# Filler order and the reversed copy: Fourier products behind the products with v, rows reversed in 16 column blocks

## The chip, the cores and the metric

The kernel runs on one core of one Trainium2 chip. The metric is the device time of one execution in microseconds (us). The engines are named as in the profile: PE is TensorE (PEld its weight loads), DVE is VectorE, ACT is ScalarE, POOL is GpSimd, SP is SyncE, which issues most of the DMAs.

## The reference: what is computed

Inputs are q, k, v of shape (4 batches, 8 heads, 576, 64). Everything is float32.

```python
scores = q @ k.T / 8                    # per batch and head, 576 x 576
scores = where(scores >= max - tau, scores, -1e9)
attn = softmax(scores);  x = (attn @ v) # heads side by side: (4, 576, 512)
u = x + real(fft(fft(x, axis=1), axis=2))
un = layernorm(u)
y = u + relu(un @ w_ch1) @ w_ch2        # 512 -> 2048 -> 512
gate = sigmoid(causal_conv5(y))
out = (gate * (y @ w_val)) @ w_out
```

## The kernel before, in words

**Attention.** Two heads make a pair; 4 batches of 4 pairs are 16 pairs. A pair has nine tiles of 128 query rows, and two tiles make a round, so there are 72 rounds. In a round PE makes the scores (`s`, L573), DVE takes the row maxima (L585) and their threshold (L588), ACT the exponentials (L592), DVE the masked probabilities and their sums (`p`, L602), POOL divides them (L609), and two rounds later PE transposes them (`t`, L643), from where ACT copies them to `m` (L652). The score buffer is free again when DVE's mask has read it, so the next scores of PE wait for the mask two tiles back.

**Fillers.** All other work of PE is put between these as filler: generators stand in five queues. `q_prep` transposes keys and queries of the next pair (L258, L268, L277). `q_tail` transposes the last 64 probability columns (L623). `q_mean` is two products for the first layer norm (L1115). `q_pv` is the products with v (L318), whose result `xt` is then folded (`g_fold`, L331) and stored to DRAM as `xs`. `q_fft` is the Fourier transform of one batch as matrix products (`g_fft`, L372), in two stages: `cdh`/`sdh` products, then `csh`/`ssh` products of 290 columns. `filler` (L678) is called twice in a round with a budget of nominal nanoseconds; `fill` (L524) takes the first queue in the order `QORD` (L47, L484) whose head is ready, and stays with one generator until it yields a name or a condition. So `QORD` alone decides which of two ready fillers stands first.

**Forced fillers.** The probability rows stand in 4 buffers. Before DVE's mask of a new row block, `emit_mask` (L595) calls `force` (L557): while the tail transposes of the block four back are not issued, it runs fillers in the same order, and the mask of DVE then waits for those transposes of PE.

**Fourier rows in reverse order.** The second half of the Fourier rows mirrors the first. `reverse` (L368) copies rows in reverse order from DRAM to DRAM with one DMA of SP: 255 rows of `xs` to `xr` when a batch is folded, and 127 and then 128 rows of `ur` to `u_d` when its sums are made (`g_add`, L449). A row has 576 floats; the DMA walks column blocks outermost, rows within.

**After attention.** When the attention loop ends, a cycle (`CYCLE`, L43) mixes what is left of the fillers with the first chunk of the MLP: `h` products (L1068) of 16 blocks of weights and `c` products (L1084). The weights come as 64-bit words and are converted in steps on DVE, ACT and POOL (L96 to L106); 18 of the 32 pieces were converted during attention, stored in DRAM as `e_h`, `e_l`, and are loaded by SP (`w0h`, ..., L863) when room becomes free. The other chunks of the MLP and the gate follow.

Of the kernel before, what the change touches and what calls it, by code (L numbers as in the profile page):

```python
# [43 lines left out]
STORE = 2  # L44
SPENT = 2
EARLY = 18
QORD = (1, 0, 4, 2, 3)  # L47
SPARE = 1.5
CHUNKS = (512,384,384,512,512)
BEHIND = 1  # L50
# [84 lines left out]
def attention_fft(tc, right, ps_f, a, u_d, dram, conv_w, hooks):  # L135
    nc = tc.nc
    PE, DVE, ACT, POOL, SP = nc.tensor, nc.vector, nc.scalar, nc.gpsimd, nc.sync
    left, right1 = ExitStack(), ExitStack()
    with ExitStack() as right2, ExitStack() as right2b, ExitStack() as right3, ExitStack() as right4, ExitStack() as scores, ExitStack() as turned:
# [227 lines left out]

        def reverse(dst, src):  # L368

            SP.dma_start(out=dst.rearrange("r (o s) -> o r s", o=2), in_=src.rearrange("r (o s) -> o r s", o=2))  # L370

        def g_fft(b):  # L372
            yield lambda: b * NP + NP - 1 in folded
            xs = xs_d.pop(b)
            rev = dram.tile([DM // 2, S], F32, name=f"xr{b}")
            SP.dma_start(out=rev[0:1], in_=xs[256:257])
            reverse(rev[1:256], xs[511:256:-1])
            boh = fft_p.tile([128, 3, DM // 2], F32R, tag="boh", name="boh")
            bol = fft_p.tile([128, 3, DM // 2], F32R, tag="bol", name="bol")
# [69 lines left out]
        def g_add(b, j, x, xr, dd, sm, ny):  # L449
            up = slice(0, HALF + 1)  # L450
            dn = slice(S - 1, HALF, -1)
            md = slice(1, HALF)
            POOL.tensor_tensor(out=x[:, up], in0=x[:, up], in1=dd[:, up], op=ALU.add)
            yield
            POOL.tensor_tensor(out=x[:, dn], in0=x[:, dn], in1=sm[:, md], op=ALU.add)
            SP.dma_start(out=u_d[b][j * 128:(j + 1) * 128], in_=x)
            yield
            if j == 0:
                ACT.activation(dd[0:1], ny, AF.Copy)
                ACT.activation(sm[0:1], ny, AF.Copy)  # L460
                yield
            POOL.tensor_tensor(out=xr[:, up], in0=xr[:, up], in1=sm[:, up], op=ALU.add)
            yield
            POOL.tensor_tensor(out=xr[:, dn], in0=xr[:, dn], in1=dd[:, md], op=ALU.add)
            rev = dram.tile([128, S], F32, name=f"ur{b}_{j}")
            SP.dma_start(out=rev, in_=xr)
            if j == 0:
                SP.dma_start(out=u_d[b][256:257], in_=rev[0:1])
                reverse(u_d[b][511:384:-1], rev[1:128])
            else:  # L470
                reverse(u_d[b][384:256:-1], rev)
            added.add((b, j))
# [10 lines left out]
        q_prep, q_tail, q_pv, q_fft, q_mean = deque(), deque(), deque(), deque(), deque()  # L483
        queues = [(q_prep, q_tail, q_mean, q_pv, q_fft)[i] for i in QORD]  # L484
        hooks.update(side=side, fillers=q_mean, fill_tile=fill_tile, done=done)
# [1058 lines left out]
```

## Time and profile before

| | us |
|---|---|
| median of 3 runs | 930.17 (928.85 to 931.04) |
| the profiled execution | 930.04, its span 928.3 |
| PE busy | 878.8 (95%) |
| DVE busy | 555.0 (60%) |
| ACT busy | 452.0 (49%) |
| POOL busy | 368.4 (40%) |
| chain that ended last | PE 36%, issue 7%, POOL 3% |

A group row of the profile gives line, engine, operation, output and inputs, the number of instructions, busy time, mean time of one in ns, and the idle time just ahead of them with what ended it. Matmuls are pipelined, so a busy PE is not PE at its peak. Idle time of an engine that is not the bottleneck costs nothing. The score and v products in float32 show two matmuls in the trace for one of the program.

### The profile page before, as it was taken

To read this page: it belongs to the slowest core of one execution; us is meant where nothing else is said; L and a number is where in the kernel's file an instruction comes from. 1 tells how busy PE (TensorE), PEld (TensorE's weight loads), DVE (VectorE), ACT (ScalarE), POOL (GpSimd) and SP (SyncE) were. 2 spreads that over 40 slices of the span, in tenths; PEclk is the share of its full clock that TensorE was granted. 3 is DMA by queue.
4 is the path that set the end of the run, shared out by engine and by line. 5 is a ranking of instruction groups with operands and counts; after the bars stand their busy time and mean duration, and the time that the engine had idled before them with its cause. 6 is when DMAs were issued, how large, how long until landed. Compare 5 with 4: busy or idle time off the path is not lost. (4 is left out here: it accounts for less than half of the span.)

```text
span 928.3 us, 14888 instructions
## 1 busy us (share of the span) xinstructions
PE 878.8 (95%) x5232; PEld 697.3 (75%) x5232; DVE 555.0 (60%) x1240; ACT 452.0 (49%) x915; POOL 368.4 (40%) x451
## 2 busy tenths in 40 slices
PE   5988898999999999899998999999999999999998
PEld 3555576657655675578876999999888878898897
DVE  6888788878877866515597445444121375525750
ACT  4778786767777765625455133233123122214432
POOL 2465544675377637612554422321110201047421
PEclk9999999999999999999999999999999999999999
DMA  6775545557455731496349723211300230333111
GB/s 154 194 191 136 154 123 149 142 174 196 138 169 162 205 101 54 137 344 208 128 152 347 278 91 126 94 71 55 110 1 1 68 125 1 116 112 130 67 44 69
DMA packets 135283, 123.34 MB, mean 133 GB/s; under 512 B 87222, under 2 KB 97702, under 8 KB 135208
## 3 DMA queue, kind: packets, MB, share of 16 engines
q1 hardware_dynamic: 126760, 97.57, 34.0%
q0 software_dynamic: 6960, 24.49, 8.5%
q8 instruction: 42, 0.69, 0.3%
q10 hardware_dynamic: 1488, 0.33, 0.2%
q14 instruction: 33, 0.27, 0.1%
HBM read 89.85 MB, written 37.22 MB: 137 GB/s over the span
## 5 line engine op out<-in xcount | busy, mean ns | idle before, releaser
L1072 DVE SCALAR_TENSOR_TENSOR hl<-h,hh 128x512 fp32r<-128x512 f32 (+1 forms) x80 | 50.9, 637 | 196.5 <-ACT hh L1071 196.5
L1071 ACT ACTIVATE hh<-h 128x512 fp32r<-128x512 f32 (+1 forms) x80 | 44.3, 554 | 250.0 <-PE h L1068 249.8
L609 POOL TENSOR_SCALAR p<-p,su 128x576 f32<-128x576 f32 x144 | 110.4, 773 | 91.7 <-DVE su L699 73.3
L602 DVE SCALAR_TENSOR_TENSOR p<-s,thr,e 128x576 f32<-128x576 f32 x144 | 112.6, 815 | 40.5 <-ACT e L592 21.0
L573 PE MATMUL s<-kt,qt 64*128 64x288 f32 (+1 forms) x640 | 100.3, 444 | 25.0 <-DVE p L602 25.0
L1084 PE MATMUL c<-hl,w1h 128*128 128x512 f32 (+1 forms) x320 | 118.0, 369 | 0.6 <-DVE hl L1072 0.6
L1084 PE MATMUL c<-hh,w1h 128*128 128x512 f32 (+1 forms) x320 | 118.0, 369 | 0.0
L1084 PE MATMUL c<-hh,w1l 128*128 128x512 f32 (+1 forms) x320 | 118.0, 369 | 0.0
L592 ACT ACTIVATE e<-s,neg 128x576 f32<-128x576 f32 x144 | 99.5, 737 | 28.7 <-DVE neg L585 28.1
L585 DVE TENSOR_REDUCE neg<-s 128x1 f32<-128x576 f32 x144 | 101.3, 744 | 15.1 <-PE s L573 15.1
L573 PEld LDWEIGHTS s<-kt,qt 64*128 64x128 f32 (+1 forms) x640 | 46.0, 177 | 66.5 <-issue 24.4
L652 ACT ACTIVATE m<-t 128x512 f32<-128x512 f32 x144 | 84.7, 588 | 6.8 <-PE t L643 6.7
L1068 PE MATMUL h<-unh,w0l 128*128 128x512 f32 (+1 forms) x320 | 79.3, 369 | 4.7 <-POOL w0l L106 4.5
L318 PE MATMUL f<-m,v 128*64 128x320 f32 (+1 forms) x512 | 81.3, 419 | 1.5 <-ACT m L652 1.2
L643 PE MATMUL t<-ident,p 128*128 128x128 f32 x576 | 79.0, 281 | 2.6 <-POOL xf L348 1.9
L1068 PE MATMUL h<-unh,w0h 128*128 128x512 f32 (+1 forms) x320 | 79.3, 369 | 1.8 <-DMA w0h<-e_h 1.0
L1068 PE MATMUL h<-unl,w0h 128*128 128x512 f32 (+1 forms) x320 | 79.2, 369 | 0.0
L643 PEld LDWEIGHTS t<-ident,p 128*128 128x128 f32 x576 | 65.5, 143 | 18.1 <-issue 10.3
L1068 PEld LDWEIGHTS h<-unh,w0l 128*128 128x128 f32 x320 | 58.4, 188 | 13.7 <-POOL w0l L106 5.8
L1084 PEld LDWEIGHTS c<-hl,w1h 128*128 128x128 f32 x320 | 60.4, 189 | 8.7 <-DVE hl L1072 1.0
L1068 PEld LDWEIGHTS h<-unh,w0h 128*128 128x128 f32 x320 | 58.4, 188 | 10.9 <-DMA w0h<-e_h 2.0
L1084 PEld LDWEIGHTS c<-hh,w1h 128*128 128x128 f32 x320 | 60.5, 189 | 7.4
(219 smaller groups left out, 1540.8 us busy)
## 6 DMA issues: line engine op xcount, KB each, us to landing
raw<-in_moe_w_ch POOLq DMA_DIRECT2D x32, 512.0 KB, 4.9
qn<-in_q SPq DMA_DIRECT2D x60, 128.0 KB, 2.9
xs<-xt SPq DMA_DIRECT2D x16, 288.0 KB, 4.1
e_h<-cx SPq DMA_DIRECT2D x18, 256.0 KB, 4.0
e_l<-ct SPq DMA_DIRECT2D x18, 256.0 KB, 4.9
w0h<-e_h SPq DMA_DIRECT2D x18, 256.0 KB, 7.2
w0l<-e_l SPq DMA_DIRECT2D x18, 256.0 KB
w1h<-e_h SPq DMA_DIRECT2D x18, 256.0 KB, 5.4
```

Source lines behind the costliest of these rows:

```text
L318: PE.matmul(out=f[h * 64:h * 64 + 64, 0:n], lhsT=w, rhs=r, start=(t == 0), stop=(t == 4))
L573: PE.matmul(out=s[o, c, 0:HALF], lhsT=qt[w, hh, q], rhs=kt[w, hh, :], start=True, stop=True)
L585: DVE.tensor_reduce(out=neg[i][:, j, 0:1], in_=sc[g][:, :, 0:HALF], axis=AX.XY, op=ALU.max, negate=True)
L592: ACT.activation(e, sc[g][:, :, 0:HALF], AF.Exp, bias=neg[g // 2][:, g % 2, 0:1], scale=1.0)
L602: DVE.scalar_tensor_tensor(out=p_view(g).rearrange("p (a b) -> p a b", a=2), in0=sc.pop(g)[:, :, 0:HALF], scalar=thr[g // 2][:, j], in1=ex ...
L609: POOL.tensor_scalar(out=v, in0=v, scalar1=su, scalar2=1.0, op0=ALU.mult, op1=ALU.mult)
L643: PE.matmul(out=f[:, t, :], lhsT=pv[:, t * 128:(t + 1) * 128], rhs=ident, is_transpose=True, start=(t == 0), stop=(t == 3))
L652: tq.append(lambda: ACT.activation(o, fv, AF.Copy))
L1068: PE.matmul(out=f[:, 0:n], lhsT=ww[:, k * 128:(k + 1) * 128], rhs=x[:, k, 0:n], start=(i == 0), stop=(i == 3 * KB - 1))
L1071: ACT.activation(hh, f[:, 0:n], AF.Relu)
L1072: DVE.scalar_tensor_tensor(out=hl, in0=f[:, 0:n], scalar=0.0, in1=f32(hh), op0=ALU.max, op1=ALU.subtract)
L1084: PE.matmul(out=ch[c][o][:, 0:n], lhsT=ww[:, o * 128:(o + 1) * 128], rhs=x, start=(at_ == 0 and i == 0), stop=(at_ == FB - 1 and i == 2))
```

## The change

Two numbers change. `QORD` puts the queues in the order tails, preparation, mean, products with v, Fourier; before, Fourier stood ahead of mean and of the products with v. And `reverse` walks 16 column blocks of 36 floats (144 B) in place of 2 of 288 floats (1152 B). The bytes moved and all arithmetic stay the same.

```diff
-QORD = (1, 0, 4, 2, 3)
+QORD = (1, 0, 2, 3, 4)
...
         def reverse(dst, src):
-            SP.dma_start(out=dst.rearrange("r (o s) -> o r s", o=2), in_=src.rearrange("r (o s) -> o r s", o=2))
+            SP.dma_start(out=dst.rearrange("r (o s) -> o r s", o=16), in_=src.rearrange("r (o s) -> o r s", o=16))
```

PE's order is the same up to the 26th round. The first place is on PE at the end of the eighth pair: the round behind its last block of scores (the `64x288` row), up to the next scores. Before:

```order
L573 MATMUL s<-kt,qt 128x288 x2
L573 MATMUL s<-kt,qt 64x288 x4
L242 MATMUL f<-ssl,boh 128x290 x3
L318 MATMUL f<-m_2067,v_197 64x256 x5
L643 MATMUL t<-ident,p 128x128 x8
L318 MATMUL f<-m_2067,v_197 64x256 x3
L318 MATMUL f<-th_256_201,vt_198 64x256 x2
L623 MATMUL f<-ident,p 64x128 x4
L318 MATMUL f<-m_2184,v_197 64x320
L573 MATMUL s<-kt,qt 128x288 x4
```

The same place in the changed kernel:

```order
L573 MATMUL s<-kt,qt 128x288 x2
L573 MATMUL s<-kt,qt 64x288 x4
L318 MATMUL f<-m_2160,v_197 64x320 x3
L318 MATMUL f<-th_320_202,vt_198 64x320 x2
L643 MATMUL t<-ident,p 128x128 x8
L623 MATMUL f<-ident,p 64x128 x4
L573 MATMUL s<-kt,qt 128x288 x4
```

Before, products of `m_2067` stand between the transposes `t` and the four tail transposes (L623); now these follow the `t` directly. `m_2067` is the first part of this pair's product with v, which is done in earlier rounds now.

The second place is on PE behind attention: the last tail transposes, the last product with v and the first two `h` blocks of the MLP. Before:

```order
L623 MATMUL f<-ident,p 64x128 x5
L318 MATMUL f<-m_4988,v_199 64x320 x8
L318 MATMUL f<-th_320_204,vt_200 64x320 x2
L1068 MATMUL h<-unh,w0h_5093 128x512 x4
L1068 MATMUL h<-unh,w0l_5094 128x512 x4
L1068 MATMUL h<-unl,w0h_5093 128x512 x4
L1068 MATMUL h<-unh,w0h_5121 128x512 x4
```

In the changed kernel:

```order
L318 MATMUL f<-m_4943,v_199 64x320 x8
L318 MATMUL f<-th_320_204,vt_200 64x320 x2
L242 MATMUL f<-csh,aeh 128x290 x3
L242 MATMUL f<-csh,ael 128x290 x3
L1068 MATMUL h<-unh,w0h_5050 128x512 x4
L1068 MATMUL h<-unh,w0l_5051 128x512 x4
L1068 MATMUL h<-unl,w0h_5050 128x512 x4
L242 MATMUL f<-csl,aeh 128x290 x3
L242 MATMUL f<-ssh,boh 128x290 x3
L242 MATMUL f<-ssh,bol 128x290 x3
L242 MATMUL f<-ssl,boh 128x290 x3
L1068 MATMUL h<-unh,w0h_5097 128x512 x4
```

Eighteen Fourier products of the third batch, which stood inside attention, now stand around the first `h` block.

The third place is SP's queue at the same time: the stores of the third batch's sums (`u_d`, `ur`) and the first weight loads. Before:

```order
L456 DMA u_d_59<-xd 128x576
L466 DMA ur_1_5006<-xr 128x576
L370 DMA u_d_59<-ur_1_5006 2x128x288
L340 DMA xs_4731<-xt 128x576
L863 DMA w0h_5093<-e_h 128x512
L863 DMA w0l_5094<-e_l 128x512
L863 DMA w1h_5095<-e_h 128x512
L863 DMA w1l_5096<-e_l 128x512
L863 DMA w0h_5121<-e_h 128x512
```

In the changed kernel:

```order
L456 DMA u_d_59<-xd 128x576
L863 DMA w0h_5050<-e_h 128x512
L863 DMA w0l_5051<-e_l 128x512
L863 DMA w1h_5052<-e_h 128x512
L863 DMA w1l_5053<-e_l 128x512
L466 DMA ur_0_5059<-xr 128x576
L468 DMA u_d_59<-ur_0_5059 16x36
L370 DMA u_d_59<-ur_0_5059 16x127x36
L432 DMA xd<-xs_3557 128x576
L433 DMA xr<-xr_4255 128x576
L863 DMA w0h_5097<-e_h 128x512
```

Before, all weight loads stand behind a reversed copy; now the first block's stand ahead of one, and the second block's behind it.

## Rows read from the trace of the kernel before

**Rows 1.** The page, its head.
```profile
span 928.3 us, 14888 instructions
```

**Rows 2.** Stretches: length, busy us of PE, PEld, DVE, ACT, POOL, granted clock, DMA.
```profile
120.00:380.00 260.00, 247.30 (x1819) 167.96 (x1817) 205.06 (x502) 187.09 (x403) 147.33 (x195) 1.00 0.51 148
380.00:400.00 20.00, 15.55 (x97) 8.94 (x94) 6.58 (x12) 9.46 (x20) 14.15 (x20) 0.91 0.52 182
400.00:480.00 80.00, 79.50 (x402) 67.16 (x401) 43.53 (x71) 35.54 (x67) 29.88 (x36) 1.00 0.59 202
480.00:512.00 32.00, 26.61 (x106) 20.39 (x106) 24.36 (x44) 19.34 (x33) 12.61 (x12) 0.95 0.88 309
512.00:900.00 388.00, 386.69 (x2018) 349.24 (x2017) 176.31 (x354) 109.59 (x206) 97.23 (x94) 1.00 0.26 87
```

**Rows 3.** Waits of PE from 120 to 386 us: total, times, longest.
```profile
PE s L573 <- DVE p L602: 9.6, 12, 1.1
```

**Rows 4.** Waits of DVE over the whole span.
```profile
DVE p L602 <- PE f L623: 11.0, 6, 2.7
```

**Rows 5.** Line L588, one in each round: times, first and last start.
```profile
L588 DVE TENSOR_REDUCE thr<-neg x72: 141/157/159, 12.6 to 382.7; 128x2 f32<-128x4 f32 x72
```

**Rows 6.** A forced round (timeline, 188 to 190 us): start, duration, instruction, idle ahead.
```profile
188.93 0.63 PE L623 MATMUL f<-ident,p 128*64 128x128 f32 x4
...
189.58 0.82 DVE L602 SCALAR_TENSOR_TENSOR p<-s,thr,e 128x576 f32<-128x576 f32 x1 [2.53 <-PE f L623]
```

**Rows 7.** PE in the two rounds behind another forced one (timeline, 242 to 248 us).
```profile
242.11 1.49 PE L573 MATMUL s<-kt,qt 64*128 64x288 f32 x8 [0.63 <-DVE p L602]
...
247.10 1.49 PE L573 MATMUL s<-kt,qt 64*128 64x288 f32 x8 [1.05 <-DVE p L602]
```

**Rows 8.** Fourier products of the second stage (timeline, 152 to 154 us).
```profile
152.00 0.56 PE L242 MATMUL f<-csh,aeh 97*2 97x290 f32 x3
152.40 0.56 PE L242 MATMUL f<-csh,ael 97*2 97x290 f32 x3
```

**Rows 9.** SP's DMA right behind a reversed copy of 255 rows (timeline of SP).
```profile
124.94 9.52 SPq L933 DMA_DIRECT2D e_h<-cx  x1
...
321.66 10.38 SPq L432 DMA_DIRECT2D xd<-xs  x1
```

**Rows 10.** DMA from 477 to 478 us, a reversed copy alone: packets, MB, share of 16 engines.
```profile
q1 hardware_dynamic: 40, 0.05, 13.3%
```

**Rows 11.** DMA from 61 to 62 us, loads in short packets.
```profile
q1 hardware_dynamic: 952, 0.23, 105.1%
```

**Rows 12.** The end of attention (timeline, 374 to 388 us).
```profile
374.36 0.59 SPq L432 DMA_DIRECT2D xd<-xs  x1
...
379.25 0.80 POOL L453 TENSOR_TENSOR xd<-xd,dd 128x289 f32<-128x289 f32 x1 [5.17 <-DMA xd<-xs]
...
383.29 0.66 PE L643 MATMUL t<-ident,p 128*128 128x128 f32 x4 [0.71 <-POOL p L609]
...
385.85 0.32 SPq L466 DMA_DIRECT2D ur<-xr  x1
...
387.56 0.63 PE L643 MATMUL t<-ident,p 128*128 128x128 f32 x4 [1.94 <-POOL xf L348]
...
387.90 0.60 SPq L370 DMA_DIRECT2D u_d<-ur  x1
```

**Rows 13.** The first weight loads and the first two `h` blocks (timeline, 390 to 403 us).
```profile
390.49 0.70 SPq L863 DMA_DIRECT2D w0h<-e_h  x1
...
394.13 0.43 SPq L863 DMA_DIRECT2D w0h<-e_h  x1
...
398.29 1.19 PE L1068 MATMUL h<-unh,w0h 128*128 128x512 f32 x4 [0.46 <-DMA w0h<-e_h]
...
402.26 1.19 PE L1068 MATMUL h<-unh,w0h 128*128 128x512 f32 x4 [0.50 <-DMA w0h<-e_h]
```

**Rows 14.** The end of the first chunk of the MLP (timeline, from 486 us).
```profile
486.63 1.20 PE L1068 MATMUL h<-unh,w0l 128*128 128x512 f32 x4 [1.85 <-POOL w0l L106]
```

## The prediction, put on record before the run

> **What bounds the kernel now.** I read the stretches first, then the waits, then the timeline at the places that the change touches. The span is 928.3 us [rows 1]; the profiled execution's own time is 930.04 us, 1.7 us around the span, and the median of the runs shown is 930.17 us, so the profile stands 0.1 us under it. PE is the engine to count. In the stretch from 120 to 380 us it is busy 247.3 of 260 us while DVE is busy 205.1; from 400 to 480 us it is busy 79.5 of 80 us, from 512 to 900 us 386.7 of 388 us [rows 2]. Only two stretches behind attention's middle have real holes: 380 to 400 us (4.45 us idle, mean granted clock 0.91) and 480 to 512 us (5.39 us idle, clock 0.95). Before 120 us the change does nothing, since PE's order is the same up to the 26th round (some 135 us). So what can be gained is what PE idles or runs slowly in some 390 us: 12.7 + 4.45 + 0.5 + 5.4 = 23 us, of which most belongs to causes that stay. One round of attention takes (382.7 - 12.6) / 71 = 5.21 us on average [rows 5].
>
> **Part 1: the order of the queues, inside attention.** With Fourier ahead of the products with v, pending tail transposes stood behind long Fourier blocks at six places, and DVE's mask waited for them: 11.0 us in 6 waits, 1.83 us each [rows 4]; one of them is the 2.53 us of [rows 6]. Walking the rules of `fill` and `force` with either table gives forced fillers in the rounds with index 26, 35, 44, 53, 62 and 68 before, and in 26, 62 and 71 now. So three of six go. That is DVE time, and DVE is not what bounds this stretch. PE works on during a forced wait, and pays behind it: with its fillers used up it waits for the mask in the next two rounds, 0.63 and 1.05 us [rows 7]. So three fewer forced rounds are worth at most 3 x 1.68 = 5.0 us on PE, and at least nothing, if other rounds are as poor in fillers. All waits of PE for the mask from 120 to 386 us come to 9.6 us in 12 [rows 3], which is the cap. The new order has about as many rounds with little filler as the old one, and its fullest round is shorter (before, one round held 18 Fourier products and more). I take 1.5 us, nearer to nothing because PE is busy 95% of this stretch anyway; as a gain, between 0 and 5.0.
>
> **Part 2: Fourier work moved behind attention.** Behind the last scores stand 135 Fourier products in place of 117, and one more product with v of the program. Three products take 0.40 us from start to start [rows 8], so 18 take 2.4 us, some 2.7 with the product with v. Attention has 2.7 us less work of PE and the stretch behind it 2.7 us more. PE is full on both sides, so the sum is nothing. Where the products now stand, around the first `h` block, PE had waited 0.46 and 0.50 us for weights [rows 13], so a little of it falls into holes. From both sides: all of it falls into the holes of 380 to 400 us (2.7 us gained), or attention is bound by DVE and does not get shorter (2.7 us lost). I take 0, in the middle of two full stretches.
>
> **Part 3: the reversed copies.** In a microsecond in which only such a copy runs, 40 packets of 1152 B take 13.3% of 16 engines: 2.1 engines, 53 ns a packet [rows 10]. So with 2 column blocks outermost a copy runs on two of sixteen engines, and 255 rows take 255 x 53 ns = 13.5 us. SP then stands: the DMA behind it takes 9.5 and 10.4 us to issue, where 0.3 to 0.6 is normal [rows 9]. With 16 blocks I expect all sixteen to share 4080 packets of 144 B. No row shows such a copy in 144 B packets; the nearest are loads in short packets, 952 packets of 0.23 MB in a microsecond that is full, 16.8 us of engine time, 17.7 ns each and some 240 B [rows 11]. At that price 255 rows take 255 x 17.7 ns = 4.5 us, 127 rows 2.2 us. At the other end, 53 ns a packet as for 1152 B, they take 13.5 and 6.7 us, on all engines. I take 17.7 ns, since the size is nearer.
> The Trainium skill, page DMA: Bandwidth & Descriptors, section Specifications, speaks against the small packets: line rate wants at least 512 B, and below that the engine reads, modifies and writes. By that rule the upper price is the likelier one, and what it does here is the third rival below. The trace bears it out in bytes per second only: 17.7 ns for 240 B against 53 ns for 1152 B is a poorer rate, but a packet is still three times cheaper.
> What does PE gain? It hardly waits for DMAs. The one place in its reach is the end of attention: `xd` is issued late at 374.4 us, behind v loads which stood behind a reversed copy; POOL waits 5.17 us for it with the divisions queued behind, and PE's transposes then wait 0.71 and 1.94 us [rows 12]. The 0.71 us names a division directly. The 1.94 us names the fold on POOL, and ACT's and DVE's own chain ends at the same time, so I leave it out. SP's stall of 9.5 us holds back the store of converted weights in the first batch, a few tenths of a microsecond of DVE at most. I take 0.7 + 0.5 = 1.2 us; between 0 and 0.71 + 1.94 + 0.5 = 3.2.
>
> **Sum.** 1.5 + 0 + 1.2 = 2.7 us gained: 930.04 - 2.7 = 927.3 in terms of the profiled execution, 927.4 in terms of the median. The end of the first chunk stays as it is: there PE waits for POOL's conversion (1.85 us of [rows 14]), in the stretch whose granted clock is 0.95; the order of the conversions relative to `h` and `c` is the same, and the Fourier work ends one `h` later with one `h` fewer behind it.
>
> **Rivals.**
> *Nothing is left of it (930.0 us).* PE bounds attention, forced waits are DVE's, and whatever PE does not do in a forced round it does in another. For it: PE 95% busy, and only 9.6 us of waits for the mask in all. Against it: the waits of [rows 7] come right behind forced rounds. It also covers the case that the copies still run on two engines. Time: 930.0, within 1 us.
> *Both holes close (922.5 us).* If the left-over Fourier work fills the hole of 380 to 400 us (2.7 us, and the clock does not fall, another 20 x 0.09 = 1.8 us), and the raw weight words come in earlier at the end of the chunk, 3 us may come on top of the 2.7: 930.0 - 2.7 - 4.5 = 922.8, or some tenths less. For it: the falls of the clock follow these very holes. Against it: the hole of 380 to 400 us is a serial chain (mask, division, transpose, copy, product with v) in which no Fourier product stands; the 18 come behind it.
> *Slower: weights behind the copy (933.5 us).* SP's queue now holds, ahead of the second `h` block's weights, the store `ur`, its wait for POOL's sums, the reversed copy and two loads. Before, that block's first load was issued at 394.1 us and PE started on it at 402.3, having waited 0.50 [rows 13]. Now POOL makes the sums behind its last divisions: from where PE's wait names it (some 387.6 us) it has five more operations of 0.8 us ahead, so some 392 to 394 us; 2 us until `ur` has landed (385.85 to 387.90 us in [rows 12]), 2 us of issues, and the load is out at 396 to 398 us. With 8 us to land, as before, it is there at 404 to 406. PE gets there at 398.3 + 3.5 (three groups of `h`, 402.26 - 0.50 - 398.29) + 2.4 = 404.2. Up to 404 nothing is lost; beyond it all is. With 2.2 us of copy on each ring in front, PE may wait 2 us, at 53 ns a packet 6 us, and after a wait of 2 us the clock is low for a few us more (1.5). Net of part of the 2.7 gained: 3.5 us lost, 933.5 us. For it: the order of SP's queue. Against it: the 8 us of landing before were themselves due to a copy on two engines just ahead (387.90 us on, 128 x 53 ns = 6.8 us), which is gone.
>
> **Chances.** Forecast (some 2.7 us gained) 0.44, nothing 0.25, both holes 0.11, slower 0.20. What a measurement of this kernel can tell from no change is about 0.2%, 1.9 us, so faster means under 928.3 and slower above 932.0. The forecast's own spread is 925 to 929.5; three quarters of it lie under 928.3. Faster: 0.44 x 0.75 + 0.11 + 0.25 x 0.1 = 0.47. Slower: 0.20 x 0.9 + 0.02 = 0.20. The rest, 0.33, is no change. The range that holds the time 8 times in 10 reaches into the second and third rival: 922.5 to 933.0.
>
> **What would show it.** Right: DVE's waits for the tail transposes fall from 6 to 3 and to some 5.5 us; the DMA behind a reversed copy on SP issues in under 5 us; a copy shows near 16 engines busy for a few us; POOL does not wait for `xd`; PE's waits for the mask from 120 us on fall by a microsecond or two; the last L588 starts some 3 to 5 us earlier than 382.7 us, and the first `h` block some 2 to 4 us earlier than 398.3. Wrong: PE's wait for `w0h` at the second `h` block grows over 1 us (third rival), the last L588 is earlier but the first chunk ends as late as before (first rival), or the waits for POOL's conversions around 486 us grow or go, which I hold fixed.

## The result and the profile after

The changed kernel is slower: 940.09 us (939.22 to 943.87, 4 runs) against 929.51 us (927.92 to 931.04, 4 runs), a ratio of 1.011 with a 95% interval of 1.0085 to 1.0134. Run again beside the experiments it gave 939.39 against 930.29 us, 1.0102 (1.0080 to 1.0124). So it loses some 10 us where the prediction gained 2.7. The time lies above the range.

The profiled execution took 943.87 us, the longest of its four runs; its span is 942.1 us. A second profile of the same kernel, from the repeat, has a span of 938.8 us, near the median, and is used beside it. The stretches of the first, to be read against [rows 2] (length, then busy us of PE, PEld, DVE, ACT, POOL, granted clock, DMA):

```profile
120.00:380.00 260.00, 246.77 (x1800) 164.28 (x1794) 203.00 (x499) 186.14 (x397) 143.92 (x193) 0.99 0.63 141
380.00:400.00 20.00, 15.48 (x97) 10.35 (x96) 4.28 (x9) 9.73 (x23) 10.91 (x15) 0.91 0.37 124
400.00:480.00 80.00, 73.18 (x365) 62.00 (x365) 37.39 (x62) 32.28 (x63) 28.29 (x33) 0.94 0.82 223
480.00:520.00 40.00, 32.23 (x118) 24.03 (x117) 24.16 (x48) 20.56 (x35) 17.14 (x17) 0.87 0.90 258
520.00:912.00 392.00, 390.19 (x2028) 351.89 (x2027) 178.42 (x360) 110.67 (x210) 97.77 (x94) 1.00 0.26 87
```

Attention is as full as before. The stretch from 400 to 480 us, which had no hole, has one of 6.8 us and a lower clock, and the end of the first chunk idles 7.8 us of 40. Stretches at fixed times blur stages that move, so from here on the time is cut at instructions: the starts of the 26th and the last L588, of the first, second and fourteenth `h` block, and of the second chunk's first `h`. In the timeline of the changed kernel these are:

```profile
129.57 0.14 DVE L588 TENSOR_REDUCE thr<-neg 128x2 f32<-128x4 f32 x1
379.77 0.16 DVE L588 TENSOR_REDUCE thr<-neg 128x2 f32<-128x4 f32 x1
396.39 1.09 PE L1068 MATMUL h<-unh,w0h 128*128 128x512 f32 x4
407.74 2.07 PE L1068 MATMUL h<-unh,w0h 128*128 128x512 f32 x4 [6.82 <-DMA w0h<-e_h]
491.65 1.20 PE L1068 MATMUL h<-unh,w0h 128*128 128x512 f32 x4
524.65 0.87 PE L1068 MATMUL h<-unh,w0h 128*128 128x384 f32 x4
```

The differences between neighbours, and the rest of the span behind, are the columns of this table. It is worked out in the same way from one profiled execution of every kernel, which need not be the median one (e8's took 926.9 us, e1's 942.6); the edits are told below, and the last column is the clock granted from 480 to 520 us. One profile is a small sample: e2 and e6 run the same program up to the last batch's copies, and their column B differs by 1.6 us.

| kernel | median us | A: round 26 to last L588 | B: to h 1 | C: to h 2 | D: to h 14 | E: to chunk 2 | rest | clock |
|---|---|---|---|---|---|---|---|---|
| before | 929.5 to 930.7 | 250.7 | 15.6 | 4.0 | 81.3 | 27.8 | 416.9 | 0.96 |
| changed | 940.09 | 250.2 | 16.6 | 11.3 | 83.9 | 33.0 | 417.4 | 0.87 |
| changed, second profile | 939.39 | 247.9 | 17.7 | 8.6 | 83.9 | 31.8 | 417.0 | 0.91 |
| e1 order alone | 945.45 | 255.0 | 16.4 | 12.8 | 82.8 | 27.2 | 416.9 | 0.96 |
| e2 16 blocks alone | 927.93 | 250.3 | 15.0 | 2.9 | 81.2 | 30.9 | 416.4 | 0.91 |
| e3 changed, one block of rows stored straight | 946.57 | 248.2 | 17.8 | 14.9 | 84.2 | 32.8 | 417.5 | 0.92 |
| e5 changed, POOL issues | 931.79 | 247.7 | 16.6 | 4.4 | 81.2 | 32.9 | 416.9 | 0.87 |
| e6 old order, last two in 2 | 925.34 | 250.3 | 13.4 | 2.9 | 81.2 | 28.1 | 416.7 | 0.96 |
| e7 changed, last two in 2 | 938.14 | 249.4 | 16.6 | 9.5 | 83.1 | 28.9 | 417.0 | 0.96 |
| e8 e5 and e7 | 930.37 | 248.1 | 16.3 | 4.4 | 81.7 | 27.9 | 417.1 | 0.96 |
| e9 old order, 4 blocks | 927.56 | 250.2 | 13.4 | 2.9 | 81.2 | 30.7 | 416.4 | 0.91 |
| e10 16 for `xr` alone | 930.24 | 250.1 | 16.7 | 4.4 | 81.2 | 27.6 | 416.5 | 0.96 |
| e11 new order, then old | 932.95 | 247.6 | 20.7 | 5.3 | 81.2 | 27.6 | 417.6 | 0.96 |
| e12 e11, POOL issues | 931.18 | 247.3 | 18.7 | 2.9 | 81.2 | 28.2 | 417.3 | 0.96 |

By the second profile the loss is -2.8 + 2.1 + 4.6 + 2.6 + 4.0 + 0.1 = 10.6 us. What is gained in attention (2.8 us) is about the work that was moved out of it (2.7 us). Columns C, D and E are most of the loss; B is 1.0 us longer in the first profile and 2.1 in the second.

Column C is one wait. SP's queue in the changed kernel (start, issue time, line, DMA):

```profile
391.91 0.38 SPq L466 DMA_DIRECT2D ur<-xr  x1
397.98 0.52 SPq L468 DMA_DIRECT2D u_d<-ur  x1
398.55 0.59 SPq L370 DMA_DIRECT2D u_d<-ur  x1
399.19 1.20 SPq L432 DMA_DIRECT2D xd<-xs  x1
400.44 0.43 SPq L433 DMA_DIRECT2D xr<-xr  x1
400.91 0.43 SPq L863 DMA_DIRECT2D w0h<-e_h  x1
```

The store `ur` goes out at 391.91, behind four weight loads of 256 KB each, and SP stands until 397.98 for it. The second block's weights go out at 400.91 and PE starts on them at 407.74, having waited 6.8 us (4.1 in the second profile). SP's own waits and PE's in this place (first SP from 385 to 412 us, then PE from 380 to 530 us; total, times, longest):

```profile
SPq L468 <- DMA ur<-xr: 5.6, 1, 5.6
```

```profile
PE h L1068 <- DMA w0h<-e_h: 6.8, 1, 6.8
PE h L1068 <- POOL w0l L106: 5.0, 3, 2.9
PE t L643 <- POOL xd L453: 3.3, 1, 3.3
```

Column D is the clock behind that wait. The group of four matmuls at 407.74 takes 2.07 us, the same group at 396.39 took 1.09. The granted clock by stretch:

```profile
405.00:410.00 5.00, 2.26 (x5) 1.82 (x6) 0.00 (x0) 0.00 (x0) 2.87 (x4) 0.50 0.98 326
410.00:415.00 5.00, 5.00 (x17) 3.93 (x16) 1.10 (x2) 0.60 (x1) 0.00 (x0) 0.68 1.05 398
415.00:420.00 5.00, 5.00 (x24) 4.14 (x23) 1.34 (x3) 0.60 (x1) 0.00 (x0) 1.00 1.06 390
```

PE stood still for 6.8 us, and the clock is at the lower level (0.50, which is 1.2 of 2.4 GHz) when it starts again. It is back before 415 us. That costs some 2.6 us (83.9 against 81.3), and it is gone where the wait is gone (e5: 81.2).

### The profile page after: what moved, and what is told of

Its sections match the earlier page's. It is cut to its first block, busy times and chain, and to the rows that moved or that the text cites. A ratio compares the mean times of both kernels' runs of the same rounds, so it can differ in the third digit from the quotient of the medians.

```text
span 942.1 us, 14906 instructions
## 1 busy us (share of the span) xinstructions
PE 881.2 (94%) x5232; PEld 696.8 (74%) x5232; DVE 548.2 (58%) x1240; ACT 453.1 (48%) x915; POOL 367.2 (39%) x451
## 4 chain that ended last, share of the span: by engine, by line
PE 67%; DVE 10%; issue 10%; POOL 5%; ACT 4%; DMA 3%; SPq 1%; DVEq 0%; POOLq 0%; ACTq 0%
PE h L1068 16%; PE c L1084 16%; PE f L318 9%; PE s L573 6%; PE o L1396 5%; PE f L242 5%; PE v L1378 4%; PE t L643 4%; DVE p L602 4%; DVE neg L585 3%; ACT e L592 1%; DMA raw<-in_moe_w_ch 1%; PE f L277 1%; PE f L623 1%; POOL res L1093 1%
## 5 line engine op out<-in xcount | busy, mean ns | idle before, releaser
L1068 PE MATMUL h<-unh,w0l 128*128 128x512 f32 (+1 forms) x320 | 81.7, 378 | 5.0 <-POOL w0l L106 5.0
L643 PEld LDWEIGHTS t<-ident,p 128*128 128x128 f32 x576 | 63.5, 140 | 20.0 <-issue 11.2
L1068 PEld LDWEIGHTS h<-unl,w0h 128*128 128x128 f32 x320 | 60.3, 193 | 8.2
```

Source lines behind the costliest of these rows:

```text
L643: PE.matmul(out=f[:, t, :], lhsT=pv[:, t * 128:(t + 1) * 128], rhs=ident, is_transpose=True, start=(t == 0), stop=(t == 3))
L1068: PE.matmul(out=f[:, 0:n], lhsT=ww[:, k * 128:(k + 1) * 128], rhs=x[:, k, 0:n], start=(i == 0), stop=(i == 3 * KB - 1))
```

## The experiments

Each was timed in five rounds beside the kernel before. In the expectations, A is the theory that the second block's weights are late because SP waits ahead of them; B, that the packets of 144 B crowd the DMA engines; C, that the moved Fourier work puts off the conversions. These letters are not those of the columns, which are called columns below.

**e1 and e2: each half of the change alone, beside the changed kernel again.** The edits are to the kernel before; e1 has the first, e2 the second.

```diff
-QORD = (1, 0, 4, 2, 3)
+QORD = (1, 0, 2, 3, 4)
...
-            SP.dma_start(out=dst.rearrange("r (o s) -> o r s", o=2), in_=src.rearrange("r (o s) -> o r s", o=2))
+            SP.dma_start(out=dst.rearrange("r (o s) -> o r s", o=16), in_=src.rearrange("r (o s) -> o r s", o=16))
```

> The changed kernel again, beside the three others on the same chip: 938 to 944 us under every theory; it says how far its own runs spread (939.2 to 943.9 so far).

> The new order of the queues with the reversed copies in 2 column blocks as before. Theory A (weights behind the copy on SP): SP's queue at the end of attention is that of the changed kernel, so the second h block waits for its weights, 6 us or more (the copy of 127 rows sits on two engines for 6.7 us), and the time is 937 to 943 us, some 8 to 13 us over before. Theory B (the 144 B packets crowd the DMA engines): no such packets, so the time is within 2 us of before, 928 to 932. Theory C (the Fourier products moved behind attention put off the conversions at the end of chunk one): some 4 to 6 us over before, 934 to 936, without the wait for w0h.

> The old order of the queues with the reversed copies in 16 column blocks. Theory A: the first weight loads stand behind the copy of 128 rows as in the kernel before, which is gone sooner, so the time is 925 to 931 us, no wait for w0h over 1 us. Theory B: the packets are those of the changed kernel, so most of its loss is there, 936 to 942 us. Theory C: 927 to 931 us.

The order alone takes 945.45 us, ratio 1.0157 (1.0133 to 1.0180). The blocks alone take 927.93 us, 0.9981 (0.9967 to 0.9996). So the order is the loss and theory B falls as its cause; the blocks even bring 0.2%. Theory C falls too, as column E of e1 is 27.2. e1's time is over theory A's band (937 to 943). Together they lose less (1.0102) than the order alone. Column A says where the time above that band comes from: with two blocks the new order takes 255.0 us from the 26th round on, with sixteen 247.9 to 250.2. In e1 SP stands behind a reversed copy (first fence, SP), and DVE, which converts weights between the rounds, waits for a store queued behind it (second, DVE):

```profile
233.95 0.60 SPq L370 DMA_DIRECT2D xr<-xs  x1
234.65 14.84 SPq L213 DMA_DIRECT2D v<-in_v  x2
...
251.18 0.55 SPq L933 DMA_DIRECT2D e_h<-cx  x1
```

```profile
255.93 0.43 DVE L96 TENSOR_SCALAR cx<-raw 128x512 int32<-128x512 int32 x1 [4.61 <-DMA e_h<-cx]
256.27 0.16 DVE L699 RECIPROCAL su<-su 128x2 f32<-128x2 f32 x1
256.35 0.74 DVE L585 TENSOR_REDUCE neg<-s 128x1 f32<-128x576 f32 x1
```

The row maxima of the round come behind that wait, and the round (the 48th) takes 10.4 us, where the changed kernel's takes 5.7. One later round, the 67th, takes 9.2 in place of 6.2. In the changed kernel the same two loads of v issue in 10.97 us.

**e3: the third batch's first rows stored straight.** The 127 rows and the one ahead of them go from the SBUF to `u_d` in the order they have, so this kernel leaves their reversal out.

```diff
-            rev = dram.tile([128, S], F32, name=f"ur{b}_{j}")
-            SP.dma_start(out=rev, in_=xr)
+            straight = (b, j) == (B - 2, 0); rev = xr if straight else dram.tile([128, S], F32, name=f"ur{b}_{j}")
+            if not straight: SP.dma_start(out=rev, in_=xr)
...
-                reverse(u_d[b][511:384:-1], rev[1:128])
+                SP.dma_start(out=u_d[b][385:512], in_=xr[1:128]) if straight else reverse(u_d[b][511:384:-1], rev[1:128])
```

> The changed kernel, but the 127 rows of the third batch's first block of sums and the row ahead of them are stored straight from the SBUF to u_d in place of the store to ur, the wait for it and the reversed copy; these rows stand in the wrong order, all else is as in the changed kernel, and PE's order is the same. Theory A: SP does not wait 5.6 us for ur, the second block's weights are issued at some 394 us in place of 400.9, PE's wait for them falls from 6.8 us to under 1 and its clock stays up: 8 to 10 us less than the changed kernel, 929 to 933 us. Theory B: one of twelve copies is gone, under 2 us less, 937 to 941. Theory C: the wait goes, the loss at the end of chunk one stays: 933 to 936.

946.57 us, 1.0171 (1.0147 to 1.0196): slower than the changed kernel, which no theory had. The edit brought a wait of its own. `xr`, which the store reads, is loaded anew right behind it:

```profile
392.53 0.23 SPq L469 DMA_DIRECT2D u_d<-xr  x1
392.85 6.04 SPq L432 DMA_DIRECT2D xd<-xs  x1
407.84 0.34 SPq L433 DMA_DIRECT2D xr<-xr  x1
408.24 0.42 SPq L863 DMA_DIRECT2D w0h<-e_h  x1
```

SP waits until 407.84 for the store to land, and PE waits 10.3 us for `w0h`. So it does not test what it was made for. It only shows that what holds SP there holds PE: the weights go out 7.3 us later than in the changed kernel (408.24 against 400.91), PE's wait is 3.5 us longer, and from the first to the second `h` block it takes 14.9 us.

**e5: another queue issues the three DMAs.** PE's order and the bytes are those of the changed kernel.

```diff
-        def reverse(dst, src):
+        def reverse(dst, src, q=SP):
...
-                SP.dma_start(out=xr, in_=rev[j * 128:(j + 1) * 128])
+                (POOL if (b, j) == (B - 2, 1) else SP).dma_start(out=xr, in_=rev[j * 128:(j + 1) * 128])
...
-                SP.dma_start(out=u_d[b][256:257], in_=rev[0:1])
-                reverse(u_d[b][511:384:-1], rev[1:128])
+                q = POOL if b == B - 2 else SP; q.dma_start(out=u_d[b][256:257], in_=rev[0:1])
+                reverse(u_d[b][511:384:-1], rev[1:128], q)
```

> The changed kernel, with three DMAs of the third batch (the row and the reversed copy of its first block of sums, and the load of xr behind them) issued by POOL in place of SP; every engine's other work is in the same order. Theory A (the second h block's weights are late because SP waits for ur ahead of them): SP issues them at some 394 to 396 us in place of 399 to 401, PE's wait for w0h falls from 4.1 and 6.8 us to under 1.5, the low clock behind it goes, and the time falls by 6 to 9 us, to 931 to 934. Rival (the copy and the loads share the engines, whoever issues them): the weights go out earlier but land as late, the wait stays at 3 to 6 us and the time at 937 to 941.

931.79 us, 1.0018 (1.0001 to 1.0035): eight of the ten microseconds are back. SP and PE now (one fence each):

```profile
390.04 0.38 SPq L466 DMA_DIRECT2D ur<-xr  x1
390.50 0.38 SPq L432 DMA_DIRECT2D xd<-xs  x1
390.94 0.47 SPq L863 DMA_DIRECT2D w0h<-e_h  x1
```

```profile
398.88 1.09 PE L1068 MATMUL h<-unh,w0h 128*128 128x512 f32 x4
```

PE no longer waits for `w0h`, and the matmuls run at full clock. The wait for `ur` is still there, 4.4 us, but on POOL, where PE does not feel it. Theory A is shown, and the rival falls: with the same transfers issued from elsewhere, columns C and D are those of before to 0.4 us. Column E stays at 32.9.

**e6, e7, e8: the last batch's two copies in 2 blocks.** e6 with the old order, e7 with the new one, e8 with e5's edit as well.

```diff
-        def reverse(dst, src):
+        def reverse(dst, src, n=16):
...
-                reverse(u_d[b][511:384:-1], rev[1:128])
+                reverse(u_d[b][511:384:-1], rev[1:128], 2 if b == B - 1 else 16)
...
-                reverse(u_d[b][384:256:-1], rev)
+                reverse(u_d[b][384:256:-1], rev, 2 if b == B - 1 else 16)
```

> The old order of the queues, 16 column blocks but for the two reversed copies of the last batch's sums, which have 2 blocks. Theory D (these two copies in 144 B packets slow the raw weight loads at the end of chunk one): from the fourteenth h block to chunk two it takes 27.8 us as before, in place of 30.9 with 16 blocks, and the time is 924 to 926. Theory E (the conversions there run at a pace of their own and end at the same time whatever is gained ahead of them): 30 us or more, 927 to 929.

> The changed kernel with the two reversed copies of the last batch's sums in 2 column blocks. Theory D: from the fourteenth h block to chunk two 27 to 28 us in place of 31.8 to 33, the time 935 to 937. Theory E: 31 us or more, 938 to 941.

> Both edits on the changed kernel: the three DMAs of the third batch on POOL, the two copies of the last batch in 2 column blocks. Theories A and D add up: 927 to 930 us. A without D: 931 to 934. D without A: 935 to 937.

e6 takes 925.34 us, 0.9951 (0.9936 to 0.9966), faster than both kernels; e7 938.14, 1.0087 (1.0066 to 1.0107); e8 930.37, 0.9985 (0.9965 to 1.0004). The median of e7 lies in the band of theory E (938 to 941), that of e8 just over the band for A and D together. Column E falls in all three pairs: 30.9 to 28.1 (e2, e6), 31.8 to 28.9 (e7), 32.9 to 27.9 (e5, e8), which is theory D's side, though e7 and e6 stay a little over its figures. By the ratios the two copies cost 0.30% (e2 to e6), 0.15% (changed to e7, intervals that overlap) and 0.33% (e5 to e8, intervals that just touch): 1.4 to 3.1 us, less than column E of single profiles says. Whether short packets are the reason is another matter.

**e9: all copies in 4 blocks of 576 B, old order. e10: 16 blocks for the copies of 255 rows alone, old order.**

> The old order of the queues with all reversed copies in 4 column blocks of 576 B. If the gain of the blocks is a copy that ends sooner, and the loss at the end of chunk one is that of short packets, four engines lie between: from the fourteenth h block to chunk two 28 to 30 us, the time 925 to 929. If only short packets matter: 28 us there, and what stands ahead of it as with 16 blocks, 923 to 926.

> The old order of the queues, 16 blocks for the copies of 255 rows (xr) alone, 2 for all copies of the sums (ur). If the gain ahead of the first weights comes from the copy of 128 rows that stands right ahead of them on SP, it is gone here: 928 to 931 us, from the last L588 to the first h block 15.6 us as before. If it comes from the copies of 255 rows: 924 to 927, as with the last two in 2 blocks.

e9 takes 927.56 us, 0.9972 (0.9959 to 0.9986), e10 930.24, 1.0008 (0.9995 to 1.0020). e9's packets are four times as long as those of 16 blocks, and its column E is 30.7, over the band of both theories, while its time is in the first one's: the length of 144 B is not what costs. What column E goes with is the clock, the last column: 0.96 in every kernel whose last two copies run in 2 blocks, 0.87 to 0.92 in every other. Cut once more, at PE's last wait for POOL's conversion, e2 and e6 show where the time goes (length, busy of PE, PEld, DVE, ACT, POOL, clock, DMA; one fence a kernel):

```profile
480.14:500.94 20.80, 13.79 (x56) 9.76 (x55) 16.49 (x27) 13.29 (x23) 10.93 (x11) 0.98 1.04 359
500.94:511.04 10.10, 10.10 (x32) 8.06 (x33) 6.03 (x11) 3.80 (x7) 2.00 (x2) 0.71 0.90 332
```

```profile
478.29:499.09 20.80, 15.23 (x56) 10.92 (x55) 16.19 (x27) 13.31 (x23) 10.90 (x11) 0.92 0.85 281
499.09:506.43 7.34, 7.34 (x33) 6.08 (x34) 5.66 (x11) 3.78 (x7) 1.32 (x2) 1.00 1.03 384
```

Up to that wait both take 20.8 us from the fourteenth `h` block: the conversions keep their own pace, as theory E had it. The 2.8 us between them are all behind it, where e2 runs at a mean clock of 0.71 and e6 at 1.00. e6 has its lower clock ahead of that wait (0.92), and does without a wait of 1.43 us for ACT's `w0h` that e2 has there. Both kernels idle 2.32 us at the same place in between (`w0l` of the fifteenth block), and the clock falls behind it in e6 and not in e2. In the changed kernel the conversions are later as well: there DVE waits 3.9 us for raw words from 502 us on in the second profile, 1.4 in e7, while e2 and e6 wait alike (2.8 and 3.1 us). So the runs of e2 and e6 show that the two copies cost time, and their profiles that e2 pays it by a lower clock behind the last conversion; what leads from a copy on more engines to that clock stays open.

e10's time is that of before, so e2's gain comes from the copies of the sums (`ur`). With these back on two engines columns B and C are 16.7 and 4.4, no better than before (15.6 and 4.0); with them on four or sixteen they are 13.4 to 15.0 and 2.9. Two things can make it. The load of `xd` stands behind v loads that stand behind a copy of 127 rows, and with it the sums, their store and the first weights come earlier. In e2 (SP):

```profile
369.67 0.58 SPq L432 DMA_DIRECT2D xd<-xs  x1
385.24 0.37 SPq L863 DMA_DIRECT2D w0h<-e_h  x1
```

Counted from the last L588, `xd` goes out 3.0 us earlier than before and these weights 3.6 us ([rows 12] and [rows 13] have 374.36 and 390.49). And the weights land 5.7 us after their issue, against 7.8 before and 8.8 in e10. PE's waits for them, 0.46 and 0.50 us in [rows 13], are gone. Either of the two would do for that, so e10 does not tell them apart.

**e11 and e12: the new order for twelve pairs, the old one behind.** Both have e6's copies; e12 also lets POOL issue `ur` and the copy of the third batch's second block.

```diff
-            t = 2 * u
+            t = 2 * u; queues[:] = queues if t < 108 else [(q_prep, q_tail, q_mean, q_pv, q_fft)[i] for i in (1, 0, 4, 2, 3)]
```

e12 alone:

```diff
-            SP.dma_start(out=rev, in_=xr)
+            (POOL if (b, j) == (B - 2, 1) else SP).dma_start(out=rev, in_=xr)
...
-                reverse(u_d[b][384:256:-1], rev)
+                reverse(u_d[b][384:256:-1], rev, 2 if b == B - 1 else 16, POOL if b == B - 2 else SP)
```

> The new order of the queues for the first twelve pairs, the old one from the 55th round on; 16 blocks but for the last two copies, 2 there. On SP no reversed copy stands between the first weight loads, as in the kernel before. If the new order saves time in the middle of attention and loses it by what it leaves for the end: L588 of the 55th round 2 to 4 us earlier counted from the 26th, no wait for w0h over 1 us, 921 to 925 us. If the new order saves nothing in attention: 925 to 928, as the old order with the same copies.

> The kernel before this one (new order for twelve pairs, then the old one, last two copies in 2 blocks) with the store ur and the reversed copy of the third batch's second block of sums issued by POOL in place of SP; there PE waited 5.8 us for the first h block's weights, which SP issued at 390.9 us behind these two. Theory A: SP issues them at 386 to 388 us, the wait falls under 2 us, the time falls by 4 to 7 us, to 926 to 929, level with or a little over the old order with the same copies (925.3). Rival (the copy's traffic or POOL's own wait for ur delays what PE needs): the wait moves to other work of PE by the same time, 931 to 934.

e11 takes 932.95 us, 1.0040 (1.0024 to 1.0057), over both of its bands. From the 26th to the 55th round it takes 154.2 us where e6 takes 157.3 and before 158.2, so the new order does shorten that part. But column B is 20.7. The third batch's sums come later, and the first block's weights stand behind their store and copy in SP's queue (PE's row, and SP's):

```profile
397.94 2.08 PE L1068 MATMUL h<-unh,w0h 128*128 128x512 f32 x4 [5.75 <-DMA w0h<-e_h]
```

```profile
388.16 0.32 SPq L466 DMA_DIRECT2D ur<-xr  x1
390.20 0.54 SPq L370 DMA_DIRECT2D u_d<-ur  x1
390.85 1.43 SPq L863 DMA_DIRECT2D w0h<-e_h  x1
```

SP waits only 1.6 us for `ur` here, as in e6 (1.7); what is late is the store itself, 10.9 us behind the last L588, where e6 issues it level with that.

e12 takes 931.18 us, 1.0018 (1.0007 to 1.0028). The weights go out at 386.54 and the wait for them is gone, but only 2 us of it come back in column B (18.7), and 2.4 in column C. POOL waits 3.7 us for `ur`, the fold `xf` stands behind it, ACT waits for the fold with the copy `th` behind that, and PE's last product with v waits for `th` (timeline of all engines):

```profile
393.36 1.07 POOL L370 DMA_DIRECT2D u_d<-ur  x1 [3.68 <-DMA ur<-xr]
394.45 0.81 POOL L346 TENSOR_TENSOR xf<-xt 128x287 f32<-128x287 f32 x1
...
395.29 0.44 ACT L351 ACTIVATE xoh<-xf 128x287 fp32r<-128x287 f32 x1 [5.44 <-POOL xf L346]
395.64 0.25 ACT L628 ACTIVATE th<-f 64x128 f32<-64x128 f32 x1
395.94 0.76 PE L318 MATMUL f<-th,vt 128*64 128x320 f32 x4 [3.67 <-ACT th L628]
```

The median lies in the rival's band: the wait for weights went, and 3.7 of its 5.8 us came back as a wait for `th`. e6 remains the fastest.

## Why the prediction was wrong

**The step that failed first** is the zero of part 2, "in the middle of two full stretches": it balanced PE's work and left out what the moved work does to SP's queue. What happened there is its own third rival, weights behind the copy, which had a chance of 0.20 and 3.5 us; columns C and D lost 10.0 us by the first profile and 7.2 by the second, where it had 3.5 net. Its place and its mechanism are shown by e5. It was held for unlikely by one comparison: the load out at 396 to 398 us, landed at 404 to 406, PE there at 404.2. Measured: out at 400.91 (399.35 in the second profile), landed at 407.7 (406.2), PE there at 400.9 (402.2). Its terms:
- `ur` was given 2 us to land, from the place before, where no weight load stood ahead of it. Behind four of them it took 6.1 us (391.91 to 397.98), and 3.2 in the second profile. The order under "The change" lists these four ahead of it, and the prediction did not price them. The traces bear this out: 2.0 to 2.1 us without them ahead (before, e2, e6, e11), 3.2 to 6.1 us with them (both profiles of the changed kernel, e1, e5, e7).
- The DMAs between `ur`'s landing and the load were given 2 us and took 2.9 (397.98 to 400.91).
- PE's arrival was set 3.3 us late (2.0 in the second profile): it took all of the 18 products as standing behind the first block, though the order shows six of them ahead, and the first block's start of before, though it forecast an earlier one.
- The 8 us for landing were near (6.8).

The clock behind the wait was put at 1.5 us and was 2.6. The sum of the second rival, which did not happen, takes off 4.5 us and leaves out the 3 us that it names at the end of the chunk.

**"The end of the first chunk stays as it is"** is the second step that failed: column E is 4 to 5 us longer, which no rival had. It comes with 16 blocks and not with the order: e2 has 3.1 of it, e1 none, and it goes with the last two copies (e6, e7, e8). By the medians it is 1.4 to 3.1 us. The way from the copies to it stays open.

**Part 1, the forced rounds.** Six waits of DVE's mask for the tail transposes were to become three. There are 7, of 10.4 us in all (8, of 11.8, in the second profile), where [rows 4] had 11.0 (waits of DVE over the whole span, then of PE from 120 to 386 us):

```profile
DVE p L602 <- PE f L623: 10.4, 7, 2.6
```

```profile
PE s L573 <- DVE p L602: 8.8, 14, 1.1
```

PE waits for the mask 8.8 us in place of 9.6 [rows 3]. The six waits of before were read as the six forced rounds, and they are not: they stand in the rounds with index 19, 35, 37, 53, 55 and 68 (at 102.8, 189.6, 199.3, 286.1, 295.8 and 367.9 us), of which three are on the list. The rounds of [rows 7] stand behind index 44, where DVE did not wait for a transpose at all, so 0.63 and 1.05 us are not the price of a forced wait. In the changed kernel the waits stand in 26, 35, 37, 44, 46, 53 and 62, where the walk gave 26, 62 and 71. The 1.5 us were not there as a gain of the whole: column A falls by 0.5 to 2.8 us, and 2.7 us of work had left. Up to the 55th round the changed kernel is 4.0 to 4.2 us ahead of before, some 0.8 of it by the blocks (e2); behind it 3.5 us of this are lost in the first profile and 1.4 in the second.

**Part 2** had the 2.7 us at zero between two full stretches, and so it came out for the work itself. What it left out is what the moved work does to the program's order, SP's queue above all. Ahead of the first `h` block, PE now makes six of the moved products and waits 3.3 us at its transposes, which the profile puts down to POOL's `xd`; before, two such waits had 0.71 and 1.94 us [rows 12].

**Part 3, the copies.** 16 engines share them, as forecast; the DMA from 124 to 126 us, where only a copy runs:

```profile
DMA packets 1705, 0.25 MB, mean 123 GB/s; under 512 B 1705, under 2 KB 1705, under 8 KB 1705
```

16 x 2 us / 1705 = 18.8 ns a packet in these two microseconds, near the 17.7 chosen. But the rate falls inside them, from 210 to 37 GB/s, and the whole copy took far longer than the 4.5 us of the forecast. Its issue, KB and time to landing:

```profile
xr<-xs SPq DMA_DIRECT2D x1, 573.8 KB, 11.3
```

Less the 2 us that `ur` takes to land alone, that is an estimate of 36 ns a packet (16 x 9.3 us / 4080), midway between the two prices. The rule of the Trainium skill cited there (page DMA: Bandwidth & Descriptors, section Specifications) is borne out in bytes per second: 123 GB/s on 16 engines is 7.7 each, the 46 GB/s of [rows 10] on 2.1 engines 22 each. The time of a copy still falls, from the 13.5 us that [rows 10] gives to some 9, since eight times as many engines work. SP's next DMA issues in 5.53 us where 9.52 stood [rows 9], not quite under 5. The gain of 1.2 us was set at PE's waits for POOL behind `xd`. In e2 `xd` does come earlier and POOL's wait for it falls from 5.2 to 2.6 us, but PE idles as long at its transposes as before (2.77 us, against 0.71 and 1.94). The two microseconds of e2 (0.19%) come at the first weights instead (e10). And the price of SP's stall was far too low with the new order, "a few tenths of a microsecond of DVE": in e1 it is 4.6 us in one round.

## What to carry to other kernels

When a change shifts work between two stages that are both full, the sum of the work is the small part. List, for the queue of every engine that issues DMAs, what now stands ahead of each load that somebody waits for, and price every transfer in front of a wait, not only the waiting one. A queue that waits for its own store holds all that follows it; another queue with time to wait takes most of it away, as long as nothing urgent is behind it there (e5 against e12).

## What had not been expected

- A store of 127 rows from the SBUF (e3) holds the next load of `xr` on SP until 407.84, 15 us behind its issue. From 402 to 406 us it is alone: packets, MB, share of 16 engines.

```profile
q1 hardware_dynamic: 44, 0.10, 6.4%
```

  That is one engine of 16, at 25 GB/s. The Trainium skill, DMA: Bandwidth & Descriptors, section Why a DMA increments its semaphore by 16 and not by 1, says that the number of engines is the largest number up to 16 that divides the slowest dimension of both sides, which is one for 127. The trace agrees, as it does for the copies with 2 blocks outermost (2.1 engines, [rows 10]).
- The clock at the end of the first chunk goes with how many engines two small copies use: 0.96 with two, 0.92 and less with four or sixteen, with nothing in PE's order changed (e2, e6, e9). These are single profiles, and the way from the copies to the clock is not shown.
